# Attention decode over cached K and V: the p·V product on four column tiles of the PE array, a fifth V tile kept on chip, wq fetched in whole rows, and a layer's transfers ending with K30 K31 V30 V31

## The chip, the cores and the metric

The kernel runs on one core of one Trainium2 chip. The metric is the device time of one execution in microseconds. The time of an execution is about 2 us above the span of its trace, because the span runs from the first to the last instruction. A ratio is the mean time of one kernel's fast runs over the mean time of the other's fast runs of the same rounds, so it is not quite the ratio of the medians that are quoted.

The engines are PE (matrix products; PEld is its weight load), DVE (vector), ACT (scalar functions), POOL, and SP, which here only issues DMA transfers.

## The reference, cut to what matters

Four layers run one after the other, A, B, A, B. Each has its own K and V cache (32 heads, 8192 positions, 192 numbers a head, bf16) and its own wq (640 x 6144) and wo (6144 x 640). A and B are each used twice.

```python
def block(x, k_cache, v_cache, wq, wo):          # x is one token, 640 numbers
    q = (x @ wq).reshape(32, 192)
    s = einsum("hd,hkd->hk", q, k) * 192 ** -0.5
    p = softmax(s)
    return einsum("hk,hkd->hd", p, v).reshape(1, 6144) @ wo

x = x + block(layernorm(x), A...)
x = x + block(layernorm(x), B...)
x = x + block(layernorm(x), A...)
x = x + block(layernorm(x), B...)
```

One head's K or V is a tile of 3.146 MB. It is used once per layer, for a single token, so nearly all of the work is moving K and V onto the chip. A layer cannot start before the last head of the layer before it is done, but its first tiles can be on chip by then.

## The kernel before: the parts that matter

On-chip memory holds eight slots of one tile each. A slot holds a K tile, a V tile, or a part of wq or wo. Transfers are issued in a fixed plan, each as soon as the slot it goes to is free. Four V tiles stay on chip from layer 0 to 2 (A) or from layer 1 to 3 (B) and are not fetched twice; while a tile stays, its slot does not rotate.

```python
NSLOT = 8
KEPT_A = (4, 12)          # heads whose V stays, layers 0 -> 2
KEPT_B = (20, 28)         # layers 1 -> 3
...
for h in range(H):                                    # the plan of one layer
    if h > 0 and (h - 1) % HEADS_W == 0 and ...:
        first(("wq", l, (h - 1) // HEADS_W))          # ten heads' columns of wq: rows of 3,840 B
    ...                                               # wo every ten heads
    first(("k", l, h))
    if l < 2 or h not in kept[l % 2]:
        first(("v", l, h))
```

One head: DVE multiplies K by q in place, in four parts. PE sums the products over d with an identity matrix. A short softmax runs over DVE, PE and ACT. Then PE forms p·V, one column of p as weights at a time, and the result stands on one PSUM partition.

```python
def head(h):
    ...
    for c in range(4):   # DVE: K *= q, a quarter of d each
        e = DV.op(lambda v, d0=d0: v.tensor_tensor(k3[:, :, d0:d0 + QD], ..., ALU.mult))
    for c in range(4):   # PE: sums over d, 24 matmuls of 512 columns
        PE.wait(chunks[c]); ...
    freed[nk] = e                                     # K's slot is free
    ...                                               # softmax -> p_sb
    PE.wait(need(nv_), ev_p, last["O"][par])
    for j in range(J):                                # J = 64 matmuls of 192 columns
        e = PE.op(lambda t, j=j: t.matmul(OB[par][0:1, 0:DH], lhsT=p_sb[par][:, j:j + 1], rhs=v3[:, j, :],
                                          start=(j == 0), stop=(j == J - 1)), signal=(j == J - 1))
    freed[nv_] = e                                    # V's slot is free
```

## Time and profile before

The median is 2049.47 us (four runs, 2046.61 to 2049.91). The traced execution took 2052.19 us.

First the page of the kernel before: granted clock, DMA share and rate in 40 equal slices of the span, then packets and the instruction queue.

```profile
PEclk9998998998899899899889989989989998997998
DMA  9999999999999999999989999999999999999994
GB/s 403 430 430 424 431 428 424 430 431 429 424 430 430 426 428 429 414 431 430 393 349 429 430 426 428 429 424 429 428 431 426 429 429 426 429 428 427 430 428 179
DMA packets 49500, 857.57 MB, mean 418 GB/s; under 512 B 4832, under 2 KB 7392, under 8 KB 15584
...
q8 instruction: 109, 1.79, 0.4%
```

The DMA runs at 424 to 431 GB/s almost everywhere: it sets the time. Three places fall short: the first slice, slices 20 and 21 (393 and 349; the boundary of layers 1 and 2) and the last slice (179). Queue q8 fetches instructions, 109 packets of 16 KB.

The groups of instructions of the kernel before that cost PE most (busy time, mean ns of one, idle time before):

```profile
L368 PE MATMUL S<-slot,ident 128*128 128x512 bf16 x3072 | 741.4, 393 | 115.6 <-DVE rl L410 67.2
L402 PE MATMUL O<-slot,p_sb 128*1 128x192 bf16 x8192 | 794.2, 264 | 0.0
```

p·V takes 5.44 us a head at full clock and mostly 7.0 to 7.7 when part of it runs at half clock (8.2 at most); the sums take 5.3. With the softmax between them PE needs 13.0 to 14.6 us a head, read from one softmax to the next, and the DMA brings a head in 14.6.

The end of the kernel before, in the timeline (start, length, engine, line, what; in brackets idle time and what ended it):

```profile
...
2019.08 3.16 PE L331 MATMUL YB<-oT,slot 128*128 128x1 bf16 x75 [0.28 <-ACT oT L326]
...
2022.17 8.04 PE L402 MATMUL O<-slot,p_sb 128*1 128x192 bf16 x64
...
2030.14 5.35 PE L368 MATMUL S<-slot,ident 128*128 128x512 bf16 x24
...
2037.68 7.09 PE L402 MATMUL O<-slot,p_sb 128*1 128x192 bf16 x64
...
2047.03 0.35 SPq L433 DMA_DIRECT2D out_dram<-x_bf  x1
```

The last tile, V31, has landed at 2026.44 us. PE is then still at V30's product, which stood behind the wo product; K31's sums, a softmax and V31's product follow. The time from the last landing to the end of the span is 23.6 us, all of it computation.

The boundary of layers 1 and 2, in windows (length; busy time of PE, PEld, DVE, ACT, POOL; granted clock; DMA share; GB/s):

```profile
1010.00:1020.00 10.00, 7.82 (x43) 3.64 (x42) 4.15 (x5) 0.62 (x3) 0.00 (x0) 0.81 0.67 261
1050.00:1060.00 10.00, 7.96 (x27) 3.01 (x27) 6.92 (x8) 0.44 (x2) 0.00 (x0) 0.76 0.61 231
1060.00:1070.00 10.00, 10.00 (x149) 8.57 (x148) 6.09 (x5) 0.90 (x3) 0.00 (x0) 0.83 0.75 301
```

Four slots are held by kept tiles there and four rotate. The next transfer waits for a slot, and the DMA engines run dry.

Transfers land in the order of their issue, so each issue's landing in the trace can be compared with the one before it. While the queue is full, a K or V tile lands 7.30 us after the transfer before it. What exceeds 7.30 us is a **late landing**. A landing counts when the slowest of the 16 DMA engines is done: V31's first engine is done at 2015.46, its last at 2026.44. Summed over all K and V tiles after the first, with the few that land a little early subtracted, late landings amount to 9.2 us between 1000 and 1095 us (the boundary) and 21.4 us elsewhere.

### The profile page before, as it was taken

The numbers are of one execution on the slowest core, as the hardware profiler recorded it, in microseconds if no ns is written. First come the engines' busy times: TensorE is split into PE (matmuls) and PEld (weight loads), VectorE is DVE, ScalarE is ACT, GpSimd is POOL, SyncE is SP. The second block draws the span as 40 slices with busy tenths as digits, with TensorE's granted clock in tenths as the row PEclk, the third lists the DMA queues.
The fourth block names the chain that finished last, engine by engine and source line by source line (L and its number), as shares of the span: only waits on it lengthen the run. The fifth ranks groups of instructions, "written<-read, shape, count | busy, mean of one in ns | idle before, by whom it ended". The sixth has DMA issues, their size and how long they took to land.

```text
span 2050.1 us, 30175 instructions
## 1 busy us (share of the span) xinstructions
PE 1669.0 (81%) x13970; PEld 1119.8 (55%) x13970; DVE 1031.3 (50%) x1071; ACT 148.5 (7%) x541; POOL 3.1 (0%) x13
## 2 busy tenths in 40 slices
PE   6887887887888788788788888878878888877887
PEld 4555545554566555555455556545555555545665
DVE  3554553555455455355446535535544654554563
ACT  0000000000000000000000000000000000000000
POOL 0000000000000000000000000000000000000000
PEclk9998998998899899899889989989989998997998
DMA  9999999999999999999989999999999999999994
GB/s 403 430 430 424 431 428 424 430 431 429 424 430 430 426 428 429 414 431 430 393 349 429 430 426 428 429 424 429 428 431 426 429 429 426 429 428 427 430 428 179
DMA packets 49500, 857.57 MB, mean 418 GB/s; under 512 B 4832, under 2 KB 7392, under 8 KB 15584
## 3 DMA queue, kind: packets, MB, share of 16 engines
q1 hardware_dynamic: 49376, 855.66, 98.0%
q8 instruction: 109, 1.79, 0.4%
q14 instruction: 15, 0.12, 0.0%
HBM read 855.64 MB, written 0.00 MB: 417 GB/s over the span
## 4 chain that ended last, share of the span: by engine, by line
PE 45%; DMA 40%; DVE 11%; ACT 2%; issue 1%; another core or an unknown queue 1%; SPq 0%; ACTq 0%; DVEq 0%
DMA slot<-in_A_k_cache_dram 23%; PE O L402 20%; PE S L368 20%; DMA slot<-in_B_k_cache_dram 17%; DVE slot L354 7%; DVE s_sb L371 2%; PE YB L331 2%; ACT p_sb L381 1%; DVE negm L379 1%; PE TB L289 1%; PE MX L376 1%; DVE m_bf L375 1%; PE MX L385 1%; PE TB L323 1%
## 5 line engine op out<-in xcount | busy, mean ns | idle before, releaser
L354 DVE TENSOR_TENSOR slot<-slot,q_sb 128x3072 bf16<-128x3072 bf16 x512 | 872.3, 1741 | 534.9 <-DMA slot<-in_A_k_cache_dram 300.8
L368 PE MATMUL S<-slot,ident 128*128 128x512 bf16 x3072 | 741.4, 393 | 115.6 <-DVE rl L410 67.2
L402 PE MATMUL O<-slot,p_sb 128*1 128x192 bf16 x8192 | 794.2, 264 | 0.0
L402 PEld LDWEIGHTS O<-slot,p_sb 128*1 128x1 bf16 x8192 | 723.9, 90 | 42.1
L368 PEld LDWEIGHTS S<-slot,ident 128*128 128x128 bf16 x3072 | 289.1, 101 | 517.0 <-DVE slot L354 190.4
L371 DVE TENSOR_REDUCE s_sb<-S 128x64 f32<-128x512 f32 x128 | 88.5, 692 | 396.6 <-PE S L368 396.6
L376 PE MATMUL MX<-ident,m_bf 128*128 128x128 bf16 x128 | 29.4, 230 | 133.6 <-DVE m_bf L375 133.6
L376 PEld LDWEIGHTS MX<-ident,m_bf 128*128 128x128 bf16 x128 | 12.3, 96 | 196.4 <-DVE m_bf L375 196.4
L385 PE MATMUL MX<-ones,l_col 128*1 128x1 f32 x256 | 24.3, 164 | 109.6 <-ACT p_sb L381 109.6
L381 ACT ACTIVATE p_sb<-s_sb,negm 128x64 bf16<-128x64 f32 x128 | 44.5, 348 | 904.5 <-DVE negm L379 904.5
L315 ACT ACTIVATE q_sb<-QB 128x192 bf16<-128x192 f32 x120 | 39.6, 330 | 774.3 <-PE QB L308 774.3
L385 PEld LDWEIGHTS MX<-ones,l_col 128*1 128x1 f32 x256 | 11.0, 81 | 127.1 <-ACT p_sb L381 127.1
L413 ACT ACTIVATE orow<-O,rl 1x192 bf16<-1x192 f32 x128 | 51.4, 402 | 129.0 <-PE O L402 67.6
L379 DVE TENSOR_REDUCE negm<-MX 128x1 f32<-128x128 f32 x128 | 37.3, 292 | 41.6 <-PE MX L376 41.6
L331 PE MATMUL YB<-oT,slot 128*128 128x1 bf16 x900 | 37.9, 178 | 3.3 <-ACT oT L326 3.3
L331 PEld LDWEIGHTS YB<-oT,slot 128*128 128x128 bf16 x900 | 36.9, 131 | 4.3 <-ACT oT L326 4.3
L308 PE MATMUL QB<-ident,qT 128*128 128x128 bf16 x240 | 31.1, 211 | 0.0
L375 DVE TENSOR_REDUCE m_bf<-s_sb 128x1 bf16<-128x64 f32 x128 | 28.5, 222 | 4.4
L289 PE MATMUL TB<-xb,slot 128*128 128x1 bf16 x900 | 26.1, 165 | 4.2 <-issue 2.8
L289 PEld LDWEIGHTS TB<-xb,slot 128*128 128x128 bf16 x900 | 25.0, 102 | 4.7 <-issue 3.1
L308 PEld LDWEIGHTS QB<-ident,qT 128*128 128x128 bf16 x240 | 13.7, 97 | 20.5 <-issue 20.5
L381 ACT ACTIVATION_READ_ACCUMULATOR p_sb<-s_sb,negm 128x1 f32 x128 | 23.8, 186 | 0.0
(37 smaller groups left out, 83.6 us busy)
## 6 DMA issues: line engine op xcount, KB each, us to landing
slot<-in_A_k_cache_dram SPq DMA_DIRECT2D x64, 3072.0 KB, 33.5
slot<-in_B_k_cache_dram SPq DMA_DIRECT2D x64, 3072.0 KB, 31.4
slot<-in_A_v_cache_dram SPq DMA_DIRECT2D x62, 3072.0 KB, 33.8
slot<-in_B_v_cache_dram SPq DMA_DIRECT2D x62, 3072.0 KB, 30.1
slot<-in_A_wq_dram SPq DMA_DIRECT2D x6, 2400.0 KB, 28.8
slot<-in_A_wo_dram SPq DMA_DIRECT2D x6, 2400.0 KB, 33.8
slot<-in_B_wq_dram SPq DMA_DIRECT2D x6, 2400.0 KB, 31.6
slot<-in_B_wo_dram SPq DMA_DIRECT2D x6, 2400.0 KB, 34.2
```

Source lines behind the costliest of these rows:

```text
L289: e = PE.op(lambda t, b=b, c=c: t.matmul(TB[:, C_QT + b:C_QT + b + 1], lhsT=t3[:, c, b * P:(b + 1) * P], rhs=xb[:, c:c + 1], start=(c == 0 ...
L331: e = PE.op(lambda t, i=i, c=c, f=y_first[0], fin=fin: t.matmul(YB[:, c:c + 1], lhsT=t3[:, i, c:D:DC], rhs=oT[:, i:i + 1], start=f, stop=f ...
L354: e = DV.op(lambda v, d0=d0: v.tensor_tensor(k3[:, :, d0:d0 + QD], k3[:, :, d0:d0 + QD], q_sb[qi][:, d0:d0 + QD].unsqueeze(1).broadcast_to ...
L368: e = PE.op(lambda t, d0=d0, fin=fin: t.matmul(S[:, :], lhsT=ident[:], rhs=k3[:, :, d0:d0 + R], start=(d0 == 0), stop=fin), signal=fin)
L371: e = DV.op(lambda v: v.tensor_reduce(s_sb[par][:], S[:].rearrange("p (j r) -> p j r", r=R), AX.X, ALU.add), e, last["s"][par])
L375: ev_m = DV.op(lambda v: v.tensor_reduce(m_bf[par][:], s_sb[par][:], AX.X, ALU.max), e, last["m"][par])
L376: e = PE.op(lambda t: t.matmul(MX[:, 0:P], lhsT=m_bf[par][:, 0:1].broadcast_to([P, P]), rhs=ident[:], start=True, stop=True), ev_m, last[" ...
L379: ev_n = DV.op(lambda v: v.tensor_reduce(negm[par][:], MX[:, 0:P], AX.X, ALU.max, negate=True), e, last["negm"][par])
L381: ev_p = AC.op(lambda a: a.activation(p_sb[par][:], s_sb[par][:], ACT.Exp, bias=negm[par][:, 0:1], accum_out=l_col[par][:]), ev_n, ev_s, l ...
L385: e = PE.op(lambda t: t.matmul(MX[0:1, C_L:C_L + 1], lhsT=l_col[par][:], rhs=ones[:, 0:1], start=True, stop=True), ev_p, ev_n)
L402: e = PE.op(lambda t, j=j: t.matmul(OB[par][0:1, 0:DH], lhsT=p_sb[par][:, j:j + 1], rhs=v3[:, j, :], start=(j == 0), stop=(j == J - 1)), s ...
L413: e = AC.op(lambda a: a.activation(orow[0:1, o0:o0 + DH], OB[par][0:1, 0:DH], ACT.Copy, scale=rl[par][0:1, 0:1]), e, ev_o, last["orow"])
```

## The change

Its intent: fetch one V tile less, waste less of the DMA on short wq rows, and make p·V and the end of a layer short enough that five kept tiles, which leave three rotating slots at the boundary of layers 1 and 2, do not starve the DMA. A row of wq is now 11,520 B in place of 3,840 B: the whole row but for the columns of the first two heads, which are fetched on their own. The core of the diff, with cuts marked (the comments in it are mine):

```diff
-KEPT_A = (4, 12)
-KEPT_B = (20, 28)
+KEPT_A = (3, 9)
+KEPT_B = (18, 23, 28)
...
+    Q_PARTS = [(c, min(2, DC - c)) for c in range(0, DC, 2)]     # wq: whole rows, 2 + 2 + 1 of 5
...
+                if h < H - 2:
+                    part = [("m", l, h), ("s", l, h), ("v", l, h)]
+                elif h == H - 2:
+                    part = [("m", l, h)]
+                else:
+                    part = [("m", l, h), ("s", l, h - 1), ("s", l, h), ("v", l, h - 1), ("v", l, h)]
+                steps += part          # m: K times q and sums, s: softmax, v: p times V
...
-                    t[:, 0:DC * HEADS_W * DH].rearrange("p (c n) -> p c n", c=DC),
-                    w["wq"][:, c0:c0 + HEADS_W * DH].rearrange("(p c) n -> p c n", c=DC))
+                    t[:, 0:k * QC].rearrange("p (c n) -> p c n", c=k),
+                    w["wq"][:, Q_FIRST * DH:].rearrange("(p c) n -> p c n", c=DC)[:, c0:c0 + k, :])
...
-                for j in range(J):
-                    e = PE.op(lambda t, j=j: t.matmul(OB[par][0:1, 0:DH], lhsT=p_sb[par][:, j:j + 1], rhs=v3[:, j, :],
-                                                      start=(j == 0), stop=(j == J - 1)), signal=(j == J - 1))
+                for m in range(J // 2):
+                    g, j = m % G, 2 * m                               # G = 4 column tiles
+                    e = PE.op(lambda e, g=g, j=j, f=m < G, fin=fin: e.matmul(
+                        OB[par][32 * g:32 * g + 2, 0:2 * DH], lhsT=p_sb[par][:, j:j + 2],
+                        rhs=t[:, j * DH:(j + 2) * DH], start=f, stop=fin, tile_position=(0, 32 * g)), ...)
...
+                ev_os[h] = ... AC.op(                                 # scaled copy of 128 x 384
+                    lambda a: a.activation(o_sb[:], OB[par][:, 0:2 * DH], ACT.Copy, scale=rl[par][:, 0:1]), ...)
+            def gather(h):            # PE adds the eight partial rows with a 0/1 column "pick"
+            def gather_last(h):       # the same for heads 30 and 31, straight into columns for wo
...
+                elif n[0] == "v":
+                    if todo is not None:
+                        todo()        # the gather of the head before
+                    values(n[2])
```

Two columns of p against two V rows of 192 columns give four products, of which two are wanted; the gather picks those and adds the four tiles. Every access to a PSUM bank by another engine is now also ordered by a wait (`bank=`).

## The prediction

> **What bounds the kernel now.** The DMA. The slice view shows the 16 engines 90% busy or more in 38 of 40 slices at about 430 GB/s, 857.57 MB in all. Taken one by one, the issues of K and V tiles land 7.30 us apart (wo slots 5.73, wq slots 6.02). 252 K/V tiles, 12 wo, 12 wq and the small loads add up to about 1990 us, plus 5 us of start. The rest of the 2050 us:
> - Landings that come late though the queue is full: about 20 us, in steps of 1.0 to 1.7 us. I read them as instruction fetches (109 packets of 16 KB, 1.07 us each) on the engine that lags most; the last tile's first engine is done at 2015.5, its last at 2026.4.
> - Layer boundary 1 to 2 (1010 to 1087): four V tiles are held, four slots rotate; the landings slip by 9 us, the timeline shows 231 to 301 GB/s for 20 us.
> - The end: 23.7 us from the last landing (2026.4) to 2050.1. The chain of waits there is all compute: V30's product waits behind wo and runs 2022.2 to 2030.2 (8.0 us at half clock), then K31's sums 5.3, softmax 2.3, V31's product 7.1, wo, out.
>
> **What the change does.**
> 1. One V tile less: -7.3 us.
> 2. wq in rows of 11,520 B instead of 3,840 B. A 3,840 B packet takes 152 ns, a 24,576 B one 915 ns; a line through both (an estimate) gives 435 ns for 11,520, against 3x152. 160 such per engine: -3.4 us.
> 3. p times V: 32 matmuls of 384 columns in place of 64 of 192, the same columns, on four column tiles. "TensorEngine Tiling (Array Packing)" of the Trainium skill, Tiling Modes, has four independent tiles at 128x32; "TensorE: Matmul & The Clock Gate", Measured speedup, 2.38x for three. No trace here shows it yet. From 5.4 to 7.1 us a head I estimate 1.5 to 2.5. PE is not the bound, so in mid-layer this is worth nothing by itself; it frees V slots 4 us earlier and takes 8,192 of 30,175 instructions away, about a quarter net of additions: fetch slips -5 us.
> 4. Boundary 1 to 2: five tiles kept leave three rotating slots. Walking it by hand (7.3 us a transfer, K's slot freed 8.5 us after landing, V's about 2 us after softmax), each issue still precedes the need by 1 to 5 us, because PV and the layer end are short. I expect most of the 9 us back: -7.
> 5. The end: order K30 K31 V30 V31. After V31 lands: 1 us behind V30's gather, PV 2, copy 0.6, gather 0.8, oT 0.3, wo 0.8, x 0.4, out 3.0: about 9 us instead of 23.7: -14.7.
> Added: gather matmuls and a 384-column ACT copy per head, reciprocal before the next head's products (about 1 us of DVE): DVE stays near 11.5 us a head, under 14.6.
>
> Sum: 2049.7 - 7.3 - 3.4 - 5 - 7 - 14.7 = 2012.
>
> **Predicted time** 2012 us, 2002 to 2025 in 8 of 10. Chances: faster by over 2% (under 2008.7) 0.30, within 2% 0.67, slower 0.03.
>
> **What would show it.** DMA about 854.4 MB; V issues 61 and 62; wq packets near 435 ns; PE under 60% busy, PV line under a third of its wall time a head; no window under 380 GB/s between 1000 and 1080; fetch packets about 80; last landing near 2003 and 8 to 10 us after it.
>
> **What would make it wrong.** Three slots starve the queue at the boundary (up to +15); column tiles don't overlap (PV stays 5 us, +3 at the end and more at the boundary); bank waits serialise PE and ACT; the lag comes from something other than fetches.

## The result, and the profile after

The changed kernel takes 2019.36 us in the median (four runs, 2018.51 to 2020.38) against 2049.47 us. The ratio is 0.9856 with a 95% interval of 0.9839 to 0.9873: about 30 us or 1.4%, inside the 2% band. The result is correct.

The page of the changed kernel, the same lines:

```profile
PEclk8887988888777788788878978888877788888888
DMA  9999999999999999999999999999999999999996
GB/s 403 430 430 430 430 429 426 430 430 429 425 432 430 429 428 430 427 430 430 407 401 415 431 428 429 430 426 430 429 429 426 431 430 430 430 429 429 430 429 292
DMA packets 44211, 854.00 MB, mean 424 GB/s; under 512 B 4816, under 2 KB 7376, under 8 KB 7888
...
q8 instruction: 82, 1.34, 0.3%
```

The bytes are down by one tile, the short packets by half, the instruction fetches from 109 to 82. Slices 20 and 21 are better but not full, and the last slice is fuller. One line moved in a way that the prediction did not foresee: the granted clock is lower, 0.832 on average against 0.914.

```profile
L396 PE MATMUL S<-slot,ident 128*128 128x512 bf16 x3072 | 849.4, 434 | 300.0 <-DVE slot L384 299.8
L433 PE MATMUL O<-slot,p_sb 128*2 128x384 bf16 x4096 | 344.3, 417 | 0.0
```

p·V takes 344 us in place of 794, but the same 3072 sums take 849 us in place of 741 (434 ns each, not 393): with less to do, PE runs them at a lower clock. (The experiment with one column tile loads PE again, and its sums take 396 ns at a mean clock of 0.923.) p·V of a head, from its first matmul to its last, has a median of 2.86 us in place of 5.44. At full clock and undisturbed it is 1.47.

The end of the changed kernel:

```profile
...
2003.03 2.40 PE L433 MATMUL O<-slot,p_sb 128*2 128x384 bf16 x32
...
2006.11 1.44 PE L463 MATMUL TB<-small,o_sb 128*64 128x1 f32 x12 [0.68 <-ACT o_sb L441]
...
2007.48 2.73 PE L433 MATMUL O<-slot,p_sb 128*2 128x384 bf16 x32
...
2010.89 1.22 PE L463 MATMUL TB<-small,o_sb 128*64 128x1 f32 x12 [0.69 <-ACT o_sb L441]
...
2013.57 0.35 SPq L511 DMA_DIRECT2D out_dram<-x_bf  x1
```

V31 has landed at 2005.42 us and 11.1 us remain. V31's product starts only at 2007.48, behind V30's product, copy and gather.

The boundary of layers 1 and 2 in the changed kernel, as a window and as lines of the timeline:

```profile
1040.00:1050.00 10.00, 7.73 (x139) 4.65 (x137) 1.64 (x5) 1.02 (x3) 0.00 (x0) 0.96 0.76 294
```

```profile
...
1033.50 6.76 DVE L384 TENSOR_TENSOR slot<-slot,q_sb 128x3072 bf16<-128x3072 bf16 x4 [2.02 <-ACT q_sb L306]
1035.32 8.07 PE L396 MATMUL S<-slot,ident 128*128 128x512 bf16 x24 [2.38 <-DVE slot L384]
1043.42 0.33 SPq L223 DMA_DIRECT2D slot<-in_A_k_cache_dram  x1
...
1054.25 6.76 DVE L384 TENSOR_TENSOR slot<-slot,q_sb 128x3072 bf16<-128x3072 bf16 x4 [8.07 <-DMA slot<-in_A_k_cache_dram]
```

The first K tile of layer 2 is on chip from 1030.51 us, but its slot comes free only after its sums, at 1043.4 us. Only then can the second K tile be issued into it. The transfer before lands at 1044.69 us, its first engine being done already at 1041.1. So the issue comes 1.3 us before that landing, and this is not early enough: the engines run dry one after the other, and the K tile lands at 1054.23, 2.24 us late.

Where the 33.6 us between the two traced executions went, read from the landings of the two traces:

| term | before | after | difference |
|---|---|---|---|
| K and V tiles at 7.30 us | 252 | 251 | -7.3 |
| first K tile landed | 13.7 | 12.4 | -1.3 |
| wq transfers, a layer | 18.02 us | 17.41 us | -2.5 in four layers |
| late landings at the boundary (1000 to 1095 us) | 9.2 | 5.1 | -4.2 |
| late landings elsewhere | 21.4 | 15.5 | -6.0 |
| last landing to end of span | 23.6 | 11.1 | -12.6 |
| sum (before rounding) | | | -33.7 |

One wq transfer of the changed kernel landed 0.5 us late; without it the wq term is -2.9.

### The profile page after: what moved, and what is told of

It reads as the page before. It is cut to its first block, busy times and chain, and to the rows that moved or that the text cites. A ratio compares the mean times of both kernels' runs of the same rounds, so it can differ in the third digit from the quotient of the medians.

```text
span 2016.5 us, 23357 instructions
## 1 busy us (share of the span) xinstructions
PE 1408.8 (70%) x10438; PEld 617.4 (31%) x10438; DVE 1047.1 (52%) x1073; ACT 217.1 (11%) x657; POOL 4.6 (0%) x22
## 2 busy tenths in 40 slices
DMA packets 44211, 854.00 MB, mean 424 GB/s; under 512 B 4816, under 2 KB 7376, under 8 KB 7888
## 4 chain that ended last, share of the span: by engine, by line
DMA 68%; PE 17%; DVE 12%; ACT 1%; issue 1%; another core or an unknown queue 0%; SPq 0%; DVEq 0%
DMA slot<-in_B_k_cache_dram 34%; DMA slot<-in_A_k_cache_dram 31%; DVE slot L384 10%; PE S L396 10%; PE O L433 3%; DMA slot<-in_A_wq_dram 3%; PE TB L448 1%; DVE s_sb L403 1%; PE YB L356 1%; ACT p_sb L413 1%; PE TB L417 1%; DVE small L410 0%; PE QM L407 0%; DVE m_bf L406 0%
## 5 line engine op out<-in xcount | busy, mean ns | idle before, releaser
L396 PE MATMUL S<-slot,ident 128*128 128x512 bf16 x3072 | 849.4, 434 | 300.0 <-DVE slot L384 299.8
L433 PE MATMUL O<-slot,p_sb 128*2 128x384 bf16 x4096 | 344.3, 417 | 0.0
L433 PEld LDWEIGHTS O<-slot,p_sb 128*2 128x2 bf16 x4096 | 128.0, 87 | 132.4 <-issue 96.1
L448 PE MATMUL TB<-o_sb,small 128*1 128x192 f32 x480 | 121.6, 386 | 36.5 <-DVE small L421 28.2
L346 ACT ACTIVATE q_sb<-QM 128x192 bf16<-128x192 f32 x120 | 39.6, 330 | 967.6 <-PE QM L339 967.6
L417 PE MATMUL TB<-small,ones 128*128 128x1 f32 x256 | 49.7, 263 | 109.6 <-ACT p_sb L413 109.6
L441 ACT ACTIVATE o_sb<-O,small 128x384 f32<-128x384 f32 x128 | 74.3, 580 | 227.2 <-PE O L433 227.2
L413 ACT ACTIVATE p_sb<-s_sb,small 128x64 bf16<-128x64 f32 x128 | 44.5, 348 | 337.5 <-DVE small L410 337.5
L417 PEld LDWEIGHTS TB<-small,ones 128*128 128x128 f32 x256 | 38.8, 191 | 129.4 <-ACT p_sb L413 129.4
L454 ACT ACTIVATE orow<-TB 1x192 bf16<-1x192 f32 x120 | 38.3, 319 | 202.6 <-PE TB L448 202.6
L448 PEld LDWEIGHTS TB<-o_sb,small 128*1 128x1 f32 x480 | 33.2, 88 | 76.3 <-DVE small L421 37.4
```

Source lines behind the costliest of these rows:

```text
L346: lambda a: a.activation(q_sb[i][:], QM[:, 0:DH], ACT.Copy), e, last["q"][i], bank=use["QM"])
L396: e = PE.op(lambda t, d0=d0, fin=fin: t.matmul(S[:, :], lhsT=ident[:], rhs=k3[:, :, d0:d0 + R], start=(d0 == 0), stop=fin), signal=fin, ba ...
L413: ev_p[h] = AC.op(lambda a: a.activation(p_sb[par][:], s_sb[par][:], ACT.Exp, bias=negm[par][:, 0:1], accum_out=l_col[par][:]), ev_n, ev_s ...
L417: e = PE.op(lambda t: t.matmul(TB[:, C_L + par:C_L + par + 1], lhsT=ones[:], rhs=l_col[par][:], start=True, stop=True), ev_p[h], last["L"] ...
L433: e = PE.op(lambda e, g=g, j=j, f=m < G, fin=fin: e.matmul(OB[par][32 * g:32 * g + 2, 0:2 * DH], lhsT=p_sb[par][:, j:j + 2], rhs=t[:, j * ...
L441: lambda a: a.activation(o_sb[:], OB[par][:, 0:2 * DH], ACT.Copy, scale=rl[par][:, 0:1]),
```

## The experiments

Unless said otherwise each is an edit of the changed kernel, and its time is compared with the changed kernel's 2019.36 us. All gave correct results. The runs are of different rounds and chips, and the changed kernel itself had medians of 2019.36 and 2017.98 us in two of them, so a difference of about 1.4 us between medians shows nothing. The ratios to the kernel before do not decide more: their intervals, which its spread of some 6 us makes wide, are 3 us to either side. By the ratios the differences that follow as +4.8, +6.6, +7.5, +1.7, -3.5 and -4.4 us are +3.3, +4.9, +5.3, +1.0, -4.3 and -5.1. The landings in the traces carry the argument, one traced execution a kernel.

**Theory.** The stream of transfers sets the time. The gain is the sum of the five terms of the prediction, and each part of the change acts through one or two of them. **Rivals.** PE relief is the main gain; the order of the last transfers is the main gain at the end; the third slot lost at the boundary eats what the fifth tile saves; the late landings elsewhere are not instruction fetches.

### Four kept tiles

```diff
-KEPT_A = (3, 9)
-KEPT_B = (18, 23, 28)
+KEPT_A = (4, 12)
+KEPT_B = (20, 28)
```

> The changed kernel with four V tiles kept (heads 4, 12 and 20, 28) as before. My theory, DMA stream bounds: one V tile more costs 7.3 us, but with four rotating slots the late landings at the boundary of layers 1 and 2 (about 5 us in the changed kernel) go, so +2 to +5 us over the changed kernel, about 2022 to 2024. Rival, three slots starve the queue by as much as the fifth tile saves: within 1 us of the changed kernel, or faster. Rival, the boundary was harmless: +7.

Measured: 2024.17 us, +4.8. The late landings at the boundary fall from 5.1 to 1.6 us, and the last landing is 4.8 us later. In the window where the changed kernel had 294 GB/s between 1040 and 1050 us, 20 us of this one read:

```profile
1040.00:1060.00 20.00, 13.32 (x157) 6.89 (x156) 8.40 (x9) 1.02 (x3) 0.00 (x0) 0.81 0.96 402
```

So the fifth tile pays, but three slots give back about 3.5 of its 7.3 us (5.1 less 1.6). The 1.6 us that are left are one step, at 1031.06, of the kind that the experiment with more instructions explains by a fetch. Theory confirmed; both rivals about the boundary fall.

### All of p·V on one column tile

```diff
-    G = 4
+    G = 1
```

> p times V with the same 32 matmuls of 384 columns a head, all on one column tile. If column tiles overlap as I think, the product of a head goes from 2 us to 5.2 us at full clock, 8 to 10 us at half clock. Theory, PE is not the bound in mid-layer: the cost is two products at the very end (+5 to +12 us after the last landing) and some starvation at the boundary of layers 1 and 2, in all +8 to +16 us, 2027 to 2035. Rival, PE relief is what made the whole change: nearly the time of before, 2045 or more. Rival, tiles do not overlap: no change.

Measured: 2088.85 us, ratio to before 1.0184 (interval 1.0167 to 1.0201, clear of 1 and just inside the 2% band). I missed by more than 50 us, and in the direction of the rival that I had not believed. The page shows why. First the chain that ended last, by engine; then the costliest PE group:

```profile
PE 77%; DVE 10%; DMA 7%; ACT 4%; issue 2%; SPq 0%; another core or an unknown queue 0%; DVEq 0%
...
L433 PE MATMUL O<-slot,p_sb 128*2 128x384 bf16 x4096 | 763.5, 350 | 0.0
```

One head's product, in the timeline of the same kernel:

```profile
619.51 5.36 PE L433 MATMUL O<-slot,p_sb 128*2 128x384 bf16 x32
```

The same 32 matmuls take 5.36 us on one tile and 1.47 us on four, both at full clock: 3.6 times. On one tile PE needs 14.1 us from softmax to softmax at full clock and 15.8 with part of it at half clock. That is more than the 14.6 us in which the DMA brings a head, where the kernel before needed 13.0 and 14.6. PE falls behind, frees slots late (19.4 us of late landings at the boundary, 26.9 elsewhere), and is 50.0 us behind at the end. The change had put about 1.2 us a head more onto PE (the gather, a larger sum for the softmax, and waits between them), and without the tiles this alone makes the kernel slower than before. "PE is not the bound" held for the kernel before only by a margin of 1.6 us a head at full clock, and of nothing in heads of which part ran at half clock.

### The last two heads in plain order

```diff
-                if h < H - 2:
-                    part = [("m", l, h), ("s", l, h), ("v", l, h)]
-                elif h == H - 2:
-                    part = [("m", l, h)]
-                else:
-                    part = [("m", l, h), ("s", l, h - 1), ("s", l, h), ("v", l, h - 1), ("v", l, h)]
+                part = [("m", l, h), ("s", l, h), ("v", l, h)]
```

> The changed kernel with the transfers and steps of a layer's last two heads in plain order K30 V30 K31 V31. Theory: after K31 lands, 7.3 us before V31, its products (8.4 us) and softmax (2.7 us) end about 4 us after V31 has landed; in the changed kernel V31's product starts 2.1 us after its landing. So only about +2 us, 2020 to 2022: most of the 12.6 us saved after the last landing came from the short product and the early wo, not from the order. Rival, the order is the main gain at the end: +8 us or more, 2027.

Measured: 2025.94 us, +6.6, between theory and rival. At the end 14.8 us follow the last landing in place of 11.1, and the boundary has 7.7 us of late landings in place of 5.1. I had counted neither the second effect nor the clock. The timeline of this kernel, where V31 has landed at 2009.13:

```profile
2003.70 7.36 PE L391 MATMUL S<-slot,ident 128*128 128x512 bf16 x24 [1.65 <-DVE slot L379]
...
2015.03 2.73 PE L428 MATMUL O<-slot,p_sb 128*2 128x384 bf16 x32
```

V31's product starts 5.9 us after its landing (2015.03 less 2009.13), because K31's sums and softmax come first. The order is worth about 3.8 us at the end and 2.6 at the boundary. Of the 12.6 us saved at the end, the larger part is not the order.

### p·V in twice as many instructions, on the same four tiles

```diff
-                for m in range(J // 2):
-                    g, j = m % G, 2 * m
+                for m in range(J):
+                    g, j = m % G, m
 ...
-                        OB[par][32 * g:32 * g + 2, 0:2 * DH], lhsT=p_sb[par][:, j:j + 2],
-                        rhs=t[:, j * DH:(j + 2) * DH], ...
+                        OB[par][32 * g:32 * g + 1, 0:DH], lhsT=p_sb[par][:, j:j + 1],
+                        rhs=t[:, j * DH:(j + 1) * DH], ...
```

> The changed kernel with p times V as 64 matmuls of 192 columns on the four column tiles: the same columns streamed, about 8,200 PE instructions more, so instruction fetches back near 109 from 82. Theory, late landings in a full queue are fetches on the slowest DMA engine: landings slip about 5 us more, the product of a head stays within 1 us of 2 us, time +4 to +7 us, about 2024 to 2026. Rival, the slips come from something else (refresh, contention at fixed times): time within 1 us of the changed kernel.

Measured: 2026.87 us, +7.5; last landing 6.8 us later. The product of a head has a median of 3.05 us against 2.86. The instruction queue on the page of this kernel:

```profile
q8 instruction: 114, 1.87, 0.4%
```

Late landings away from the boundary are 21.0 us, against 15.5 with 82 fetches and 21.4 in the kernel before with 109. They follow the number of fetches, not the kernel, and most come in steps of 1.0 to 1.5 us where one 16 KB packet takes 1.07 us. The packet records tie the steps to fetches one by one. Up to 1035 us, the steps of over 0.3 us of the changed kernel stand at the tiles during which its 1st, 9th, 17th, 25th, 33rd and 41st fetch ran; those of this kernel at its 1st, 9th and so on to the 57th, and with four kept tiles it is every eighth fetch to the end of the kernel. The other fetches up to there leave no such step. After the boundary of layers 1 and 2, it is mostly one or two in every eight. What fits is that fetches go round the DMA engines and that only those on the engine which is last by then delay a landing; the trace does not name a packet's engine, so this part is inferred. The fetches are 0.4% of the DMA's time by the page, but the landing of a tile waits for the slowest engine, and its delay is not made up for while the queue is full. The theory is confirmed, the size a little above my range. The two traced executions are 9.0 us apart, more than the medians: about 5.6 us are in these landings, 1.5 at the boundary and 2.2 after the last landing.

### wq in runs of 3,840 B again

```diff
+                for g in range(3):
+                    a = Q_FIRST * DH + g * (QC // 3)
+                    e = SP.op(lambda s, g=g, a=a: s.dma_start(
+                        t[:, g * k * (QC // 3):(g + 1) * k * (QC // 3)].rearrange("p (c n) -> p c n", c=k),
+                        w["wq"][:, a:a + QC // 3].rearrange("(p c) n -> p c n", c=DC)[:, c0:c0 + k, :]), ...)
 ...   # the single transfer is taken out, and the matmuls of wq read the three parts
```

> The changed kernel with the same wq bytes and slots, but fetched in runs of 3,840 B (each wq transfer as three of a third of the columns). Theory: packets go from 434 ns per 11,520 B to 3 x 152 ns per 11,520 B, so the wq transfers of a layer take 18.1 us in place of 17.3, in all +3 us, about 2022. Rival, row length does not matter: within 1 us of the changed kernel.

Measured: 2021.03 us, +1.7; last landing 2.5 us later. By the packet records of the two traces, a 3,840 B packet takes 152 ns in the kernel before and an 11,520 B one 434 ns in the changed kernel, so three short ones cost 22 ns more, and 160 such on each engine make 3.5 us. The time shows about half of it, which is no more than the changed kernel differs from itself between rounds, so the time alone does not confirm it. The traces do in direction: the wq transfers add up to 71.7 us in place of 69.6, while 0.6 of the 2.5 us are a first K tile that landed later.

### The kernel before with five kept tiles and nothing else

```diff
-KEPT_A = (4, 12)
-KEPT_B = (20, 28)
+KEPT_A = (3, 9)
+KEPT_B = (18, 23, 28)
```

> The kernel before with only the five kept V tiles of the change (heads 3, 9 and 18, 23, 28), all else as before. Saves 7.3 us of transfer. Theory: with p times V on one tile and the late layer end, three slots starve the queue at the boundary of layers 1 and 2 far more than four did (9 us of late landings before), and PE, which needs 13 to 15 us a head, cannot catch up: the saving is lost, 2047 to 2062. Rival, five tiles pay for themselves alone: 2042 to 2044.

Measured: 2051.36 us against 2050.41 in the same rounds, ratio 1.0006 (interval 0.9991 to 1.0022). The slices of its page at the boundary:

```profile
GB/s 402 429 429 427 429 430 424 429 429 427 428 430 429 426 428 431 417 431 426 343 344 414 431 425 429 429 422 429 430 429 406 430 429 429 429 427 427 429 429 247
```

Slices 20 and 21 are at 343 and 344 GB/s; late landings at the boundary are 18.1 us in place of 9.2. The 8.9 us lost there swallow the 7.3 saved: the last landing is 1.6 us later (2027.99 against 2026.44). The traced execution was the fastest of the four, 2047.44 us. Its last two products took 6.73 and 5.44 us where the traced execution of the kernel before needed 8.04 and 7.09 by the clock, and only 17.3 us follow its last landing in place of 23.6. So the fifth tile is worth nothing in the kernel before. With the changed kernel's gain of 4.8 us from it, this is the interplay that the change rests on; which of its parts makes the difference, the shorter p·V or the shorter end of the layer, was not tested apart.

### A remedy for the end: V31's product before V30's gather

The scaled product of the last head gets its own buffer, laid over the output row, which is free then.

```diff
+        o_two = orow_all[:, 0:4 * DH].bitcast(F32)
 ...
-                    if todo is not None:
-                        todo()
-                    values(n[2])
+                    if n[2] < H - 1:
+                        if todo is not None:
+                            todo()
+                        values(n[2])
+                    else:
+                        values(n[2])
+                        todo()
```

> The changed kernel with a second buffer for the scaled product of the last head (laid over the output row, which is free then), and V31's product issued before V30's gather. In the changed kernel V31's product starts 2.1 us after V31 has landed because it stands behind V30's copy and gather. Theory: it starts with the landing, V30's gather overlaps V31's copy, and the end shortens by 1 to 1.5 us at each layer end; the time falls by 1 to 3 us, 2016 to 2018.

Measured: 2015.89 us, -3.5, a little more than expected. The timeline of its end, where V31 has landed at 2002.32 us:

```profile
2001.04 2.79 PE L435 MATMUL O<-slot,p_sb 128*2 128x384 bf16 x64
...
2007.96 0.35 SPq L519 DMA_DIRECT2D out_dram<-x_bf  x1
```

Both products run as one piece (64 matmuls) and 8.9 us follow the last landing. The boundary gains too: late landings of 2.4 us in place of 5.1, because the second K tile of layer 2 is issued at 1040.45 us in place of 1043.42. Not all of that is the order: the first products of layer 2 start 1.5 us earlier (1031.96 against 1033.50), and from there to the end of their sums it is 8.5 us in place of 9.9, in a stretch (1020 to 1040) whose clock was 0.67 in this execution, 0.51 in the changed kernel and 0.50 in its repeat. How much of the gain at the boundary the order would bring at the same clock is open.

### A remedy for the clock: dummy matmuls in PE's waits

```diff
+            def warm(n, b=None):                 # identity times identity into an unused bank
+                b, u = (QT, "QT") if b is None else b
+                for i in range(n):
+                    PE.op(lambda t: t.matmul(b[:, :]..., lhsT=ident[:], rhs=ident[:]..., start=True, stop=True), ...)
 ...   # in softmax, heads 30 and 31 only: warm(3) before the maximum, warm(4) before the sum
 ...   # in layer 2, after the first part of wq: warm(22, (YB, "YB"))
```

> The changed kernel with dummy matmuls (identity, result never read) in the softmax waits of the last two heads and, in layer 2, after the first part of wq. In the changed kernel the granted clock is 0.5 from 2004 to 2010 and from 1020 to 1040, after PE sat idle for softmax. Theory: with the idle time filled the clock stays up, V31's product takes 2.0 us in place of 2.7 and the first K products of layer 2 free their slots 1 to 1.5 us earlier, so late landings at the boundary shrink; time -2 to -4 us. Rival, half clock follows something else than PE idle time: no change in the clock, time the same or +1.

Measured: 2014.99 us, -4.4, a little more than expected. The boundary in windows, first the changed kernel, then this one (the clock is the third number from the end):

```profile
1020.00:1040.00 20.00, 14.86 (x118) 7.50 (x107) 7.73 (x14) 2.23 (x6) 0.54 (x1) 0.51 1.00 428
1040.00:1060.00 20.00, 11.66 (x149) 6.10 (x148) 7.38 (x9) 1.02 (x3) 0.00 (x0) 0.76 0.87 355
```

```profile
1020.00:1040.00 20.00, 14.86 (x136) 8.09 (x136) 8.17 (x15) 2.25 (x7) 0.54 (x1) 0.83 0.99 423
1040.00:1060.00 20.00, 16.42 (x170) 7.68 (x168) 8.14 (x8) 1.02 (x3) 0.00 (x0) 0.83 0.99 406
```

The clock in the first window is 0.83 in place of 0.51, the second K tile of layer 2 is issued at 1040.49 us, 2.9 us earlier, and late landings at the boundary are 2.9 us. At the end itself the gain is not shown: 10.7 us follow the last landing, and the next run shows that the clock can be up there without any remedy.

### The changed kernel again, and both remedies together

The last three ran on one chip with five rounds. The third adds 24 dummy matmuls after the last part of wq in layer 2.

> The changed kernel again, on the same chip as the next two. Nothing is altered: it should be within 2 us of its first 2019 us, with late landings of 1 to 2 us at the boundary of layers 1 and 2 and about 11 us after the last landing.

> The changed kernel with both remedies: second buffer and V31 before V30's gather, and dummy matmuls in the softmax waits of the last two heads and after the first part of wq in layer 2. Theory, the two remedies overlap in part (V31's product also ran at full clock when it came earlier): last landing near 2002, 8 to 9 us after it, time 2012 to 2015, 5 us or so under the changed kernel on the same chip. Rival, they do not add: 2015 to 2016.

> As the one with both remedies, with 24 more dummy matmuls after the last part of wq in layer 2, where the clock is still 0.5 before the third head's K. Theory: that head's products free their slot about 1 us earlier, but the queue is by then barely starved, so 0 to -1 us against both remedies; if the dummies run into the head's products it is +1 to +3 us.

Measured: the changed kernel 2017.98 us (2017.73 to 2018.58), ratio 0.9848 to before; both remedies 2014.51 us (2013.21 to 2015.08), ratio 0.9830; with more dummies 2014.33 us (2013.47 to 2014.95), ratio 0.9830. The changed kernel repeats: 5.4 us of late landings at the boundary (the expectation says 1 to 2, though the first trace already had 5.1), 10.1 us after the last landing. In this execution V31's product ran at full clock:

```profile
2008.24 1.47 PE L433 MATMUL O<-slot,p_sb 128*2 128x384 bf16 x32
```

It started 2.4 us after the landing at 2005.88 and took 1.47 us, not 2.73. So half clock at the end comes and goes between executions of one kernel, and is worth about 1 us there; the late start is in both.

Both remedies together are no better than either beyond about 1 us, which is nearer to the rival than to the 5 us that I expected: the last landing is at 2002.3 to 2002.8 us in all of them, and 8.6 to 9.0 us follow it wherever V31's product goes first. They act on the same wait, the slot of layer 2's first K tile (issue of the second at 1040.45, 1040.49 and 1040.46 us). The kernels with both are the fastest that I ran: the first of them is 3.5 us under the changed kernel on the same chip with ranges that do not overlap, and 34.5 us under the kernel before. More dummies gave nothing, as expected.

## Why the prediction was right or wrong

The prediction was 2012 us with a range of 2002 to 2025, and 67% for a change within 2%. Measured were 2019.36 us and 1.4%: inside the range, and the likeliest class. The mechanism was right; the sum was 7.4 us too hopeful. Term by term:

- **One tile less, -7.3: right.** 251 tiles in place of 252. Four kept tiles cost 4.8 us: 7.3, less the 3.5 that the boundary returned, plus 1.4 of late landings elsewhere, about 0.4 less in other terms.
- **wq rows, -3.4: right.** The packet took 434 ns (estimated 435), the landings gained 2.5 to 2.9 us. Undoing it cost 2.5 us in the last landing; the 1.7 us of time are within what differs between rounds.
- **Fewer fetches, -5: right.** Late landings away from the boundary fell by 6.0 us, and doubling the p·V instructions brought 5.6 us back.
- **The boundary, -7: mis-sized.** It returned 4.2. The step that failed is "each issue still precedes the need by 1 to 5 us, because PV and the layer end are short". I had walked it with K's slot free "8.5 us after landing" and a layer end of about 9 us; the trace has first products 11.5 us after V31's landing (1033.50 less 1021.97), and sums that end 9.9 us after the products start, most of it at half clock. Nor is preceding the need by 1 us enough, if the need is the landing of the transfer before: the second K tile of layer 2 preceded it by 1.3 us and was 2.24 us late. In the twelve traces with unsplit wq transfers, all 15 K and V tiles that were issued less than 2 us before the landing of the transfer before came 2.1 to 6.4 us late, and with each remedy alone, at leads of 4.4 us, the same tile came 0.02 and 0.67 us late. An estimate from these: about 4 us of lead are needed here. Moving the issue forward by 3 us, by either remedy, took the late landings from 5.1 to 2.4 or 2.9 us.
- **The end, -14.7: mis-sized.** It was -12.6 in the traced execution and -13.5 in the repeat. The step is "1 us behind V30's gather, PV 2": V31's product started 2.1 and 2.4 us after the landing. V30's product cannot start before V31's softmax is issued, since both softmaxes follow K31's products on DVE, and the copy and gather come after that. The product itself took 2.73 or 1.47 us, by the clock. Part of the -12.6 is the clock too: the end of the kernel before was traced once, with its last two products at 8.04 and 7.09 us, partly at half clock.
- **"PE is not the bound, so in mid-layer this is worth nothing by itself": wrong as a statement about the change.** I had costed what the tiles take away from PE, but I looked at the added gather only for DVE. With the additions and no tiles, PE needs 14.1 to 15.8 us a head against 14.6, and the kernel takes 2088.85 us.
- **What the profile would show.** Bytes (854.00 MB), V issues (62 and 61), wq packets and fetches (82) came as said. "PE under 60% busy" failed (70%), "under a third of its wall time a head" failed (2.86 of 5.44 us; 1.47 only at full clock), and "no window under 380 GB/s" failed (294 from 1040 to 1050). All three failed for a common reason in part: relieved of work, PE ran at a lower clock, 0.832 against 0.914. The last landing "near 2003" was at 2005.42, and "8 to 10 us after it" were 11.1.

Of the 7.4 us, 3.8 are these terms (37.4 predicted, 33.6 between the traces, which include 1.3 us at the start that the prediction does not have). The other 3.5 is that I subtracted from the median what I had read in an execution that was 2.7 us slower than the median, and the traced execution after is 0.8 us below its own. Why executions of the kernel before spread from 2046.2 to 2052.2 us was not examined. The clock at the end may be part of it: the same code, in the trace with five kept tiles, ran its last two products 3.0 us faster in all.

**Pages and traces.** "TensorEngine Tiling (Array Packing)" of the Trainium skill, Overview, gives up to 4 times for a small dimension of at most 32; this case has 3.6 times (5.36 to 1.47 us). "TensorE: Matmul & The Clock Gate", Part 1, describes a clock that halves after an idle window of about 3.4 us and a window that runs freely of the kernel. The traces agree on the window: the clock records hold only the values 0.5 and 1, half clock lasts whole multiples of 3.41 us but for the last of a trace, and the end of the changed kernel (2003 to 2010 us) had 0.53 in one execution and 1.00 in the repeat. They do not agree on idle: the last section has the numbers. "Runtime: NRT & Kernel Launch", Instruction fetch mechanics, has instructions come in blocks of 16 KiB, 256 instructions each; the trace has packets of that size, and 8,192 more PE instructions brought 32 more of them (114 against 82).

## What to carry to other kernels

When the DMA sets the time, ask of every change when it lets the next transfer be issued and what still runs after the last landing, and judge the fetches of its instructions as transfers on the slowest DMA engine. Cost what a change adds to an engine that is "not the bound" against the margin that this engine has, here nothing to 1.6 us a head, by the clock. A transfer must be issued well before the one ahead of it has landed, here about 4 us by the estimate above. Parts of a change can be worthless alone and pay together: five kept tiles gained nothing in the kernel before and 4.8 us in the changed one.

## What the Trainium skill lacked or had wrong

- "Runtime: NRT & Kernel Launch", Instruction fetch mechanics, calls the cost of crossing a block "mostly hidden". It is not where the DMA is the bound: 32 more blocks (114 against 82) put the last landing 6.8 us later, about 5.6 of it in late landings, mostly steps of 1.0 to 1.5 us at every eighth fetch. No page gives a time for what a fetch costs a full queue.
- "DMA: Bandwidth & Descriptors", Specifications, gives 512 B as the size from which transfers run at line rate. Here rows of 3,840 B took 152 ns (25.3 B a ns), rows of 11,520 B 434 ns (26.5), rows of 24,576 B 914 ns (26.9): 6% between the first and the last.
- The same page does not say how far engines drift apart in one long queue: the first engine was done with the last tile 11.0 us before the last engine (2015.46 and 2026.44), and a consumer waits for the last.
- "TensorE: Matmul & The Clock Gate", Part 1, gives an idle window of about 3.4 us as what halves the clock. Here the clock mostly fell without one: in the 3.41 us before a fall PE was busy for 37% of the time and its longest idle stretch was 1.05 us (medians over the changed kernel; 44% and 1.04 us over the kernel before). So relieving PE of work slowed the work that was left with idle stretches of about 1 us: the same 3072 sums took 434 ns each in place of 393, at a mean granted clock of 0.832 in place of 0.914, and 396 ns at 0.923 when one column tile loaded PE again.
